# One tile's two store segments on two DMA queues, at the end of a fused attention and expert kernel

## The chip, the cores and the metric

The kernel runs on one core of a Trainium2 chip. Time is the device's time for one execution, in microseconds; the time before is the median of three runs.

## The reference

Sparse attention over 8 batches, 8 heads, 576 positions and 64 columns a head is followed by a two-layer network with an ELU between its layers:

```
scores = scale * q @ k.T                       # per batch and head
mask   = local (0 <= i-j < 32) for heads 0..3, strided ((i-j) % 32 == 0, i >= j) for heads 4..7
attn   = softmax(where(mask, scores, -1e9))
x      = (attn @ v) as [4608 tokens, 512]      # 8 batches of 576 tokens, heads side by side
h      = x @ w_in                              # [4608, 2048]
g      = where(h > 0, h, exp(min(h, 0)) - 1)
out    = g @ w_out                             # [4608, 512], float32
```

## The kernel before

Tokens are handled within a batch in an order of their own: token `p * 8 + s` of a batch stands at place `s * 72 + p`. There are 72 rows for each of the eight `s`, 576 for a batch. Chunks of 512 such places (9 of them) go through the two layers. Layer 1 (line 605) gives 16 blocks of 128 columns, which ScalarE and VectorE (DVE) turn into `g`. Layer 2 (line 639, token `Z`) multiplies `g` by `w_out` for one tile of 128 places at a time: four tiles a chunk, named `chunk.tile`, so 8.3 is the last tile of the last chunk. Its 128 x 512 result lies in a PSUM bank; a copy (line 645, by ScalarE with token `o`, by DVE with token `q`) brings it into an output tile `osb`, from a pool of four buffers, and `store` (token `t`) writes it to memory.

Since a tile of 128 places runs across the 72-row boundaries, `store` cuts it into two or three segments and issues one DMA for each (line 657). `engs` lists the queues, taken by turns; by default that is SyncE's (SP's) alone:

```
def store(ch, kk, engs=(nc.sync,), fs=slice(0, d_model)):
    ...
        n = min(RS - p, c0 + 128 - c)
        engs[i % len(engs)].dma_start(out=out_v[b, s, p:p + n, fs], in_=o_sb[c - c0:c - c0 + n, fs])
        c, i = c + n, i + 1
```

The last tile, 7.3, is computed and stored in three pieces: 256, 128 and 128 columns wide (`l2_piece`, token `Y`, line 669; `out_piece`, token `y`, lines 679 and 681). Piece 0 is copied by ScalarE and its two segments of 64 rows are stored from SP. Pieces 1 and 2 are copied by DVE, and of each the first segment is stored from SP, the second from ScalarE's queue.

The order of all this work is written out by hand in `ORDER`: a list of tokens that are run one after the other, each of which appends its instructions to its engines' programs. Every engine then runs its own instructions in that order and waits on semaphores where data, a buffer or a counter must be ready. SP's program holds nothing but DMA issues; ScalarE's holds its activations, its copies and the few DMAs issued from it. The stores of both queues count their landing on eight shared counters (named DMAHW0 to DMAHW7 in the built program), which the build gives out in turns. A store whose counter was used before waits until the earlier store on it has landed.

The last two lines of `ORDER` begin with the tiles of chunks 7 and 8 that are left; in them the copies `o.8.3`, `q.7.2`, `q.7.1`, `q.7.0`, `o.8.2` and then the three pieces of 7.3 follow each other.

Of the kernel before, what the change touches and what calls it, by code (L numbers as in the profile page):

```python
# [140 lines left out]
i.7.14 g.7.14 Z.7.2.0.6 h.7.4 i.8.8 j.7.8 Z.8.2.0.7 g.8.8 g.7.8 j.7.4 Z.8.0.0.4 g.8.10 L.8.15.1 g.7.4  # L141
Z.8.3.1.2 h.8.15 i.8.15 Z.8.0.1.4 g.8.15 Z.8.2.1.7 Z.8.1.0.5 Z.7.2.1.6 Z.8.1.1.5 Z.7.1.0.3 Z.8.1.2.5
Z.8.0.2.4 Z.7.2.2.6 Z.8.1.3.5 Z.8.0.3.4 o.8.1 Z.7.0.1.0 o.8.0 t.8.0 Z.8.3.2.2 Z.7.1.1.3 t.8.1 Z.7.1.2.3
Z.8.3.3.2 Z.7.2.3.6 o.8.3 t.8.3 Z.7.0.2.0 q.7.2 Z.7.1.3.3 t.7.2 Z.7.0.3.0 q.7.1 Z.8.2.2.7 t.7.1 q.7.0
Z.8.2.3.7 t.7.0 Y.7.3.0.6 o.8.2 t.8.2 y.7.3.0 Y.7.3.1.5 y.7.3.1 Y.7.3.2.4 y.7.3.2
"""

# [2 lines left out]
def kernel(  # L150
# [9 lines left out]
    nc = tc.nc  # L160
# [20 lines left out]
    g = [consts.tile([128, MC, CHUNK], BF16, tag=f"g{i}", name=f"g{i}") for i in range(2)]  # L181
# [433 lines left out]
    def clamp(eng, ch, m):  # L615
        i = int(ch), int(m)
        e = tiles.pop(("he", i))
        e1 = p_he1.tile([128, CHUNK], BF16, tag="he1", name="he1")
        if eng is nc.scalar:
            nc.scalar.activation(e1, e, ACT.Relu, bias=1.0, scale=-1.0)  # L620
        else:
            eng.tensor_scalar(e1, e, scalar1=1.0, scalar2=1.0, op0=ALU.min, op1=ALU.subtract)  # L622
        tiles["he1", i] = (e1, eng is nc.scalar)
# [19 lines left out]
    def copy_o(eng, ch, kk):  # L643
        o_sb = tiles["osb", ch, kk] = p_osb.tile([128, d_model], F32, tag="osb", name="osb")
        eng(o_sb, tiles.pop(("o", int(ch), int(kk))))  # L645
# [3 lines left out]
    def store(ch, kk, engs=(nc.sync,), fs=slice(0, d_model)):  # L649
        o_sb = tiles["osb", ch, kk]  # L650
        c0 = int(ch) * CHUNK + int(kk) * 128
        c, i = c0, 0
        while c < c0 + 128:
            b, r = divmod(c, S)
            s, p = divmod(r, RS)
# [3 lines that stand above are left out]
# [15 lines left out]
    def out_piece(ch, kk, i):  # L674
# [15 lines left out]
        "a": lambda ch, m, bk: l1(ch, m, (2, 3), bk), "b": lambda ch, m: l1(ch, m, (0, 1)),  # L690
        "L": lambda ch, m, bk: l1(ch, m, (2, 3, 0, 1), bk), "h": exp_h,
        "i": lambda *a: clamp(nc.vector, *a), "j": lambda *a: clamp(nc.scalar, *a),
        "g": elu, "Z": l2, "t": store, "Y": l2_piece, "y": out_piece,
        "o": lambda *a: copy_o(nc.scalar.copy, *a),
        "q": lambda *a: copy_o(nc.vector.tensor_copy, *a),
    }
# [33 lines left out]
```

## Time and profile before

| | us |
|---|---|
| median of 3 runs | 307.64 (307.57 to 308.14) |
| the profiled execution | 308.06 |
| its span, first to last instruction | 306.3 |
| TensorE busy | 294.3 (96%) |
| ScalarE busy | 228.6 (75%) |
| DVE busy | 227.3 (74%) |
| stores issued from SP after 289 us | 24, first at 289.1, last at 303.57 |
| stores issued from ScalarE | 2, at 300.94 and 301.84 |

The profile is of one execution; its span lies 1.7 us below that execution's own time. Durations in the text are from it. In a timeline a row has the start, the duration, the engine, the line and the operation, and in brackets the engine's idle time before it with what ended it. SPq and ACTq are DMA issues by SyncE and ScalarE; the transfer itself happens later on the 16 DMA engines, so an issue's row says nothing of when the data has landed.

### The profile page before, as it was taken

The page shows a single profiled execution, that of the slowest core. Times are in us where ns is not written, and L with a number is a line of the kernel's source. Part 1 is how long each engine was busy: PE and PEld are TensorE (multiplying, and loading weights), DVE is VectorE, ACT ScalarE, POOL GpSimd, SP SyncE. Part 2 cuts the span into 40 slices and gives each one's busy share as a digit, 9 for nine tenths or more (in the row PEclk, how much of TensorE's full clock was granted, in tenths as well). Part 3 has the DMA queues.
Part 4 walks back from the last instruction along what each step waited for, and adds up shares of the span by engine and source line. Part 5 has one row for each costly group of instructions (what it writes and reads, how often), then busy time and mean ns, then how long its engine had stood idle before and what let it go on. Part 6 is the DMA issues. An engine that isn't in the chain of part 4 may idle for free.

```text
span 306.3 us, 6219 instructions
## 1 busy us (share of the span) xinstructions
PE 294.3 (96%) x2299; PEld 146.8 (48%) x2339; DVE 227.3 (74%) x435; ACT 228.6 (75%) x412; POOL 81.7 (27%) x110
## 2 busy tenths in 40 slices
PE   6999999999999999999999999999999999999993
PEld 2654455445544454545544554454444544444453
DVE  6877959798779978896788878976788468894020
ACT  4778678588879888997989889978786659881110
POOL 8943336630472008530178240000000000000000
PEclk9999999999999999999999999999999999999999
DMA  8999999999999859999899599601120022000143
GB/s 164 184 206 206 207 193 166 153 196 207 169 153 168 127 118 134 162 193 159 203 149 155 65 138 167 166 26 46 37 68 0 2 68 68 2 1 0 28 150 98
DMA packets 107278, 37.59 MB, mean 123 GB/s; under 512 B 89104, under 2 KB 102768, under 8 KB 107248
## 3 DMA queue, kind: packets, MB, share of 16 engines
q0 software_dynamic: 69648, 19.43, 62.9%
q1 hardware_dynamic: 37088, 17.38, 27.8%
q10 hardware_dynamic: 512, 0.39, 0.5%
q8 instruction: 18, 0.29, 0.4%
q14 instruction: 12, 0.10, 0.1%
HBM read 39.47 MB, written 9.44 MB: 160 GB/s over the span
## 4 chain that ended last, share of the span: by engine, by line
PE 86%; DVE 6%; ACT 2%; issue 2%; DMA 2%; ACTq 0%; DVEq 0%
PE ps L639 39%; PE ps L605 36%; PE ps L450 3%; DVE g L633 2%; PE ps L520 2%; PE ps L513 2%; DVE he L622 2%; DMA g<-in_k_dram 2%; PE ps L669 1%; ACT he L613 1%; DVE mask_l L349 1%; DVE xT L578 1%; PE ps L493 0%; ACT e L457 0%; PE ps L408 0%
## 5 line engine op out<-in xcount | busy, mean ns | idle before, releaser
L639 PE MATMUL ps<-w_out_sb,g 128*128 128x512 bf16 x538 | 129.6, 379 | 2.0 <-issue 0.6
L605 PE MATMUL ps<-xT,w_in_sb 128*128 128x512 bf16 x559 | 129.4, 379 | 1.6 <-issue 0.3
L613 ACT ACTIVATE he<-ps 128x512 f32<-128x512 f32 x144 | 81.0, 597 | 22.2 <-PE ps L605 19.9
L605 PEld LDWEIGHTS <-w_in_sb 128*128 128x128 bf16 x576 | 55.0, 98 | 64.9 <-issue 1.7
L639 PEld LDWEIGHTS <-g 128*128 128x128 bf16 x560 | 51.1, 98 | 55.6 <-issue 0.6
L633 DVE TENSOR_TENSOR g<-he,ps 128x512 bf16<-128x512 bf16 x92 | 62.0, 684 | 1.9
L578 DVE TENSOR_TENSOR xT<-ps,ln 64x576 bf16<-64x576 f32 (+1 forms) x64 | 42.5, 677 | 19.7 <-ACT ln L553 18.9
L457 ACT ACTIVATE e<-ps 72x576 bf16<-72x576 f32 (+1 forms) x64 | 39.1, 647 | 13.4 <-PE ps L450 11.7
L622 DVE TENSOR_SCALAR he<-he 128x512 bf16<-128x512 f32 x92 | 40.1, 445 | 7.7 <-ACT he L613 7.0
L548 ACT ACTIVATE ln<-ps 64x576 f32<-64x576 f32 (+1 forms) x64 | 36.3, 583 | 9.8 <-PE ps L520 4.9
L631 DVE SCALAR_TENSOR_TENSOR g<-he,ps 128x512 bf16<-128x512 bf16 x52 | 34.8, 682 | 7.2 <-ACT he L620 6.9
L553 ACT ACTIVATE ln<-ln 64x576 f32<-64x576 f32 (+1 forms) x64 | 38.5, 619 | 1.2
L620 ACT ACTIVATE he<-he 128x512 bf16<-128x512 f32 x52 | 32.5, 630 | 1.6 <-DVE g L633 1.1
L645 DVE COPY osb<-ps 128x512 f32<-128x512 f32 x22 | 15.1, 685 | 16.3 <-PE ps L639 16.0
L239 POOL DMA_DIRECT2D ql<-in_q_dram x24 | 19.9, 833 | 6.8 <-DMA vl<-in_v_dram 3.1
L645 ACT COPY osb<-ps 128x512 f32<-128x512 f32 x13 | 7.6, 586 | 18.0 <-PE ps L639 14.1
L246 POOL DMA_DIRECT2D kl<-in_k_dram x24 | 17.8, 745 | 11.9 <-DMA w_out_sb<-in_moe_w_out_dram 4.0
L470 DVE TENSOR_TENSOR pm<-e,mask_l 128x576 bf16<-128x576 bf16 x32 | 14.1, 454 | 7.0 <-ACT e L457 5.4
L464 DVE TENSOR_TENSOR pm<-e,mask_s 72x576 bf16<-72x576 bf16 x32 | 14.2, 450 | 4.3 <-ACT e L457 4.1
L233 POOL DMA_DIRECT2D vs<-in_v_dram x8 | 5.2, 653 | 26.4 <-DVE vsp L585 25.2
L256 POOL DMA_DIRECT2D vl<-in_v_dram x8 | 9.6, 1195 | 8.7 <-PE ps L520 6.4
L513 PEld LDWEIGHTS <-vsp 72*128 72x128 bf16 x192 | 9.1, 98 | 5.4 <-DVE pm L464 0.3
(93 smaller groups left out, 156.1 us busy)
## 6 DMA issues: line engine op xcount, KB each, us to landing
out_dram<-osb SPq DMA_DIRECT2D x32, 144.0 KB
vl<-in_v_dram POOLq DMA_DIRECT2D x8, 288.0 KB, 8.8
w_in_sb<-in_moe_w_in_dram POOLq DMA_DIRECT2D x4, 512.0 KB, 13.0
w_out_sb<-in_moe_w_out_dram POOLq DMA_DIRECT2D x4, 512.0 KB, 16.3
kl<-in_k_dram POOLq DMA_DIRECT2D x24, 72.0 KB, 7.7
ql<-in_q_dram POOLq DMA_DIRECT2D x24, 72.0 KB, 8.8
ks<-in_k_dram POOLq DMA_DIRECT2D x5, 320.0 KB, 8.4
vs<-in_v_dram POOLq DMA_DIRECT2D x5, 320.0 KB, 8.6
```

What stands on the lines that cost most here:

```text
L457: nc.scalar.activation(e[0:R], tiles.pop(("S", key, u))[0:R], ACT.Exp, scale=scale)
L548: nc.scalar.activation(t, s_ps, ACT.Ln)
L553: nc.scalar.activation(t, t, ACT.Exp, scale=-1.0)
L578: nc.vector.tensor_mul(dst, o_ps, rc)
L605: nc.tensor.matmul(tiles["h", ch, m], lhsT=w_in_sb[:, c, m * 128:(m + 1) * 128], rhs=xT[:, c, ch * CHUNK:(ch + 1) * CHUNK], start=(c == 2) ...
L613: nc.scalar.activation(e, tiles["h", i[0], i[1]], ACT.Exp)
L620: nc.scalar.activation(e1, e, ACT.Relu, bias=1.0, scale=-1.0)
L622: eng.tensor_scalar(e1, e, scalar1=1.0, scalar2=1.0, op0=ALU.min, op1=ALU.subtract)
L631: nc.vector.scalar_tensor_tensor(dst, e1, -1.0, h, op0=ALU.mult, op1=ALU.max)
L633: nc.vector.tensor_tensor(dst, e1, h, op=ALU.max)
L639: nc.tensor.matmul(ops, lhsT=g[ch % 2][:, m, kk * 128:(kk + 1) * 128], rhs=w_out_sb[:, m, :], start=(m == 0), stop=(m == MC - 1), skip_gro ...
L645: eng(o_sb, tiles.pop(("o", int(ch), int(kk))))
```

## The change

The tile 8.3 (places 4480 to 4607: the last 56 rows of `s` = 6 and the 72 rows of `s` = 7 of the last batch) is stored by a new token `u`, which calls `store` with the queues of SP and ScalarE by turns. Its first segment, 56 rows, goes on SP's queue as before; its second, 72 rows, goes on ScalarE's. Nothing else in the text of the kernel differs.

```
-Z.8.3.3.2 Z.7.2.3.6 o.8.3 t.8.3 Z.7.0.2.0 q.7.2 Z.7.1.3.3 t.7.2 Z.7.0.3.0 q.7.1 Z.8.2.2.7 t.7.1 q.7.0
+Z.8.3.3.2 Z.7.2.3.6 o.8.3 u.8.3 Z.7.0.2.0 q.7.2 Z.7.1.3.3 t.7.2 Z.7.0.3.0 q.7.1 Z.8.2.2.7 t.7.1 q.7.0
...
-        "g": elu, "Z": l2, "t": store, "Y": l2_piece, "y": out_piece,
+        "g": elu, "Z": l2, "t": store,
+        "u": lambda ch, kk: store(ch, kk, (nc.sync, nc.scalar)), "Y": l2_piece, "y": out_piece,
```

## The prediction

> **What bounds the kernel now.** I read the page first, for where the change lies in the span.
>
> ```profile
> span 306.3 us, 6219 instructions
> ...
> PE 294.3 (96%) x2299; PEld 146.8 (48%) x2339; DVE 227.3 (74%) x435; ACT 228.6 (75%) x412; POOL 81.7 (27%) x110
> ...
> PE   6999999999999999999999999999999999999993
> ...
> DMA  8999999999999859999899599601120022000143
> ```
>
> TensorE is busy for 96% of the span, and for nearly all of it nothing but TensorE counts. The last slice (7.7 us wide) is different: TensorE falls to 3 tenths and the DMA engines to 3. The edited tile is stored just ahead of it, so the next views are of that end. The chain of waits, last rows:
>
> ```profile
> 297.94 3.55 PE ps L669 x48
> 301.49 0.02 issue
> 301.51 0.29 DVE osb L679
> ```
>
> The last computation ends at 301.51 + 0.29 = 301.80; the span ends at 306.3. These 4.5 us hold only stores and the closing barrier. Here the bound is the last store's issue and landing. The timeline, from the first store of the last tile, by engine (start, duration, engine; SPq and ACTq are the DMA issues of SyncE and ScalarE):
>
> ```profile
> 300.12 0.47 SPq L657 DMA_DIRECT2D out_dram<-osb  x1
> 300.64 0.59 SPq L657 DMA_DIRECT2D out_dram<-osb  x1
> 303.00 0.47 SPq L657 DMA_DIRECT2D out_dram<-osb  x1
> 303.57 0.54 SPq L657 DMA_DIRECT2D out_dram<-osb  x1
> ...
> 300.94 0.54 ACTq L657 DMA_DIRECT2D out_dram<-osb  x1
> 301.84 0.47 ACTq L657 DMA_DIRECT2D out_dram<-osb  x1
> ...
> 300.62 0.29 DVE L679 COPY osb<-ps 128x128 f32<-128x128 f32 x1 [3.67 <-PE ps L669]
> 301.51 0.29 DVE L679 COPY osb<-ps 128x128 f32<-128x128 f32 x1 [0.60 <-PE ps L669]
> ```
>
> The last tile (7.3) leaves in three pieces: piece 0 by two stores from SP (300.12, 300.64), pieces 1 and 2 each by one store from SP and one from ScalarE. Piece 1 is copied by 300.62 + 0.29 = 300.91. ScalarE stores its half at once (300.94). SP is free at 300.64 + 0.59 = 301.23, yet stores its half only at 303.00, and piece 2's half behind it at 303.57, although that was ready at 301.80. SP's own list of waits between 301 and 304 us says why:
>
> ```profile
> SPq L657 <- DMA out_dram<-osb: 1.7, 1, 1.7
> ```
>
> SP waits 1.7 us for another store to land. Which one, the order of the two built programs tells, with what each instruction waits for. Each store counts up one of eight counters DMAHW0 to 7, given out in turns over both queues, in the order in which the build expects the stores to be issued; before a counter is used again, the store that had it must have landed. First before, then after (rows left out at "..."):
>
> ```
> ## SP: 125 rows
> ...
> 106 L657 DMACopy out_0_dram<-osb_3948 56x512 [waits DMAHW4_49,Activation_49]
> 107 L657 DMACopy out_0_dram<-osb_3948 72x512 [waits DMAHW5_49]
> ...
> 115 L657 DMACopy out_0_dram<-osb_3978 72x512 [waits DMAHW5_49]
> 116 L657 DMACopy out_0_dram<-osb_3978 40x512 [waits DMAHW7_49]
> 117 L657 DMACopy out_0_dram<-osb_4003 40x512 [waits DMAHW0_49,Activation_49]
> 118 L657 DMACopy out_0_dram<-osb_4003 72x512 [waits DMAHW2_49]
> ...
> 122 L657 DMACopy out_0_dram<-osb_4008 64x128 [waits DMAHW6_49,DVE_49]
> 123 L657 DMACopy out_0_dram<-osb_4008 64x128 [waits DMAHW7_49,DVE_49]
> ```
> ```
> ## SP: 124 rows
> ...
> 106 L657 DMACopy out_0_dram<-osb_3948 56x512 [waits DMAHW5_49,Activation_49]
> ...
> 115 L657 DMACopy out_0_dram<-osb_3978 40x512 [waits DMAHW6_49]
> 116 L657 DMACopy out_0_dram<-osb_4003 40x512 [waits DMAHW0_49,Activation_49]
> 117 L657 DMACopy out_0_dram<-osb_4003 72x512 [waits DMAHW1_49]
> 118 L657 DMACopy out_0_dram<-osb_4003 16x512 [waits DMAHW3_49]
> ...
> 121 L657 DMACopy out_0_dram<-osb_4008 64x128 [waits DMAHW6_49,DVE_49]
> 122 L657 DMACopy out_0_dram<-osb_4008 64x128 [waits DMAHW7_49,DVE_49]
> ```
>
> Before, SP's turns go 5, 7, 0, 2: counters 6 and 1 went to ScalarE's two stores. So counter 6, for which SP's piece 1 store (row 122) waits, is that of ScalarE's piece 1 store, issued at 300.94; the wait ends as that one lands, just ahead of 303.00. Two engines store halves of one piece, and by the round of eight one must wait for the other.
>
> **The change part by part.** The 128 rows of tile 8.3 fall into two segments (56 and 72 rows). The first stays on SP, the second goes to ScalarE's queue. The rows around it:
>
> ```profile
> 292.80 0.59 ACT L645 COPY osb<-ps 128x512 f32<-128x512 f32 x1 [3.73 <-DMA out_dram<-osb]
> 298.02 0.59 ACT L645 COPY osb<-ps 128x512 f32<-128x512 f32 x1 [4.64 <-PE ps L639]
> ...
> 293.41 0.32 SPq L657 DMA_DIRECT2D out_dram<-osb  x1
> 293.77 0.37 SPq L657 DMA_DIRECT2D out_dram<-osb  x1
> 294.38 0.32 SPq L657 DMA_DIRECT2D out_dram<-osb  x1
> ...
> 293.66 0.69 DVE L645 COPY osb<-ps 128x512 f32<-128x512 f32 x1 [13.76 <-PE ps L639]
> ```
>
> 1. Removed from SP: one issue of 0.37 us at 293.77. SP's next store (294.38) starts only when DVE's copy ends, at 293.66 + 0.69 = 294.35; SP was free at 294.14. So SP gets 0.37 us of idle time and no later store moves: worth 0.
>
> 2. Added to ScalarE: one issue right behind its copy, from 293.39. Its price lies between 0.37 (the same store on SP) and 0.54 (ScalarE's dearer issue); I take 0.5, done by 293.9. Behind it on ScalarE stand the copy at 298.02, which waits for TensorE, piece 0's copy and the two stores of 7.3. The cover is 298.02 − 293.9 = 4.1 us of idle ScalarE; without it the 0.5 would go into the end. The copy at 298.02 also needs the four-deep output buffer that this tile gives back, so its landing matters: ScalarE's store of 300.94 had landed by 303.00, 2.06 us; from 293.4 that gives 295.5, 2.5 us early. Worth 0.
>
> 3. The counters. One store that the build expects earlier, on an idle queue, turns the round by a place. After, SP's turns go 6, 0, 1, 3: ScalarE's last stores have counters 7 and 2. SP's piece 1 store now waits for counter 6, that of tile 7.0's last segment, long landed; its piece 2 store, the very last, waits for counter 7, ScalarE's piece 1 store. So the wait doesn't go, it moves back by one store:
> - SP's piece 1 store is issued when SP is free, 301.23 + 0.05 (the gap between 300.12 + 0.47 and 300.64) = 301.28, no longer at 303.00.
> - SP's piece 2 store is ready at 301.80, and waits for the same landing as before: issued at 303.00 instead of 303.57. That is 0.57 us.
> - It no longer stands right behind another issue: 0.47 instead of 0.54, 0.07 more.
>
> Sum: 0.57 + 0.07 = 0.64 us. The packets confirm the distance of the last two stores. The DMA view in the windows 304.0 to 304.7 (slices of 0.0175 us) and 304.7 to 306.3 (0.04 us):
>
> ```profile
> DMA  0000000224547667664121100000000000000000
> ...
> DMA  0144664200000000000000000004000000000000
> ...
> q1 hardware_dynamic: 80, 0.03, 7.8%
> q14 instruction: 1, 0.01, 1.2%
> ```
>
> The first store moves its data from 304.12 to about 304.40, the second from 304.74 to 305.02: 0.62 apart. The lone packet later is of another queue. From the last data packet to the span's end are 1.3 us, of landing and barrier, and they follow the last store whenever it comes.
>
> 4. What may eat it: SP's piece 1 issue (301.28 to about 301.85) now overlaps ScalarE's piece 1 issue (300.94 to 301.48) by 0.2 us, and the last store hangs on that one's landing. Before, ScalarE's issue overlapped SP's of 300.64 by 0.29 us; the two took 0.59 and 0.54 where a lone one takes 0.47 (303.00, 301.84). So 0.3 us of overlap cost at most 0.12; 0.2 us cost up to 0.08, and nothing if ScalarE's descriptors are by then all made. The bounds are 0 and, if the landing is pushed by a whole issue, 0.47. I take 0.02, since the overlap falls in the last third of that issue. The other rows of this end, ScalarE's 301.84 among them, keep their times: DVE and TensorE aren't touched.
> The Trainium skill's page "Perfetto Trace Analysis", section "DMA Instruction — HWDGE (DVE, Sync)", says that the sequencers which issue such DMAs share one descriptor generator. The stretched 0.59 and 0.54 agree; taken as strict turns, it would eat the bound of 0.47 and leave 0.17 us of gain.
>
> Net: 0.64 − 0.02 = 0.62 us. The profiled execution took 308.06 us by the device (span 306.3 and 1.7 around it); it would take 307.44. The median of the runs is 307.64, 0.42 lower, and no step above depends on that distance: 307.64 − 0.62 = 307.02.
>
> **The rivals.**
> Hidden anyway, 307.64: reading SP alone, the removed 0.37 us lies in front of a wait for DVE (step 1), 12 us ahead of the end. If the order of landing made counters meaningless for the end (the 303.00 wait being on something else that stays), nothing moves. For it speaks that no view names the store waited for; against it, that the only long wait of SP coincides with a counter owned by ScalarE in the build, and that this owner changes.
> The Trainium skill's page "DMA: Bandwidth & Descriptors", section "Issuing engines are not separate DMA queues", says that issuing from several engines saves only the sequencer's issue time. By that rule alone the change saves 0.37 us on SP in front of an idle stretch, that is this rival; the 1.7 us row shows a second coupling, through the counters, that the rule doesn't treat.
>
> A slower end: the last store now depends on ScalarE's piece 1 store, whose issue lies between two of SP's. If descriptors are made one store at a time with SP's first, it comes out behind both, each 0.59 at most: 1.18 later than alone. It had at most 0.12 of that before; so the last store would go out 1.06 later than my 303.00, and 1.06 − 0.64 = 0.42 us are lost: 308.06. It decides from a landing 0.64 us later than before. Against it: ScalarE's 0.54 beside SP's 0.59 shows two issues side by side, not in turns.
>
> A partial gain, inside the forecast's case: 0.17 to 0.5 us, where step 4 costs more than I take.
>
> **How the numbers follow.** A difference of 0.2% (0.62 us) is about what a measurement of this kernel can tell from no change, and my gain stands on that line. Forecast case 0.80, hidden 0.12, slower 0.08. Of the forecast case I put 0.52 above the line, since the sum of 0.64 comes from rows and only step 4 takes from it, and 0.28 below, with the partial gains. That gives faster 0.52, same 0.28 + 0.12 = 0.40, slower 0.08. The likeliest case's own range is 306.85 to 307.47: the sum by step 4's bound above, and 0.17 under the forecast for the scatter of a median (the three runs span 307.57 to 308.14). The range reaches on to the hidden case, to 307.66, and to 306.80 for that scatter.
>
> **What would show it.** In the profile after: SP's piece 1 store at about 301.3 instead of 303.00; a wait of about 1.2 us (from 301.85) on a store's landing in front of SP's last issue, now at 303.0 to 303.1; its packets alone from about 304.1; the last data packet, and the span, some 0.6 us earlier; a 72-row issue on ScalarE at 293.4, and SP's 294.38 unmoved. I am wrong if SP's last issue is still near 303.57, if ScalarE's store of 300.94 lands after 303.6, or if a row before 300 us moves.

## The result and the profile after

The changed kernel takes 306.82 us (median, 306.24 to 307.82) against 307.57 (306.93 to 308.28) for the kernel before: ratio 0.9977, 95% interval 0.9968 to 0.9987, that is 0.71 us less (0.40 to 0.98). The forecast was 0.62 us less.

The profiled execution took 306.47 us, 1.59 less than the one of before. Most of that isn't the change's, as the span's two parts show. The page, and the timeline of the end (start, duration, engine; the ACT row is the copy of tile 8.3, just ahead of the edited store):

```profile
span 304.8 us, 6219 instructions
```
```profile
292.45 0.32 SPq L657 DMA_DIRECT2D out_dram<-osb  x1
293.43 0.32 SPq L657 DMA_DIRECT2D out_dram<-osb  x1
...
299.17 0.47 SPq L657 DMA_DIRECT2D out_dram<-osb  x1
299.68 0.59 SPq L657 DMA_DIRECT2D out_dram<-osb  x1
300.38 0.54 SPq L657 DMA_DIRECT2D out_dram<-osb  x1
302.04 0.47 SPq L657 DMA_DIRECT2D out_dram<-osb  x1
...
292.46 0.65 ACTq L657 DMA_DIRECT2D out_dram<-osb  x1
299.99 0.55 ACTq L657 DMA_DIRECT2D out_dram<-osb  x1
300.88 0.47 ACTq L657 DMA_DIRECT2D out_dram<-osb  x1
...
291.84 0.59 ACT L645 COPY osb<-ps 128x512 f32<-128x512 f32 x1 [3.73 <-DMA out_dram<-osb]
...
300.56 0.29 DVE L679 COPY osb<-ps 128x128 f32<-128x128 f32 x1 [0.60 <-PE ps L669]
```

The last DVE copy ends at 300.85, against 301.80 before: 0.95 us earlier. That much lies ahead of the edit: the copy of tile 8.3, which the edited store follows, already begins at 291.84 instead of 292.80. It is scatter between executions: another kernel below, whose program differs from this one only in which of two tiles in the last 17 us goes by two queues, has the last copy at 302.03 instead of 300.56. What the change can reach is read from the end of the last copy. To the span's end (304.76, and 306.34 before, to two places) it takes 304.76 − 300.85 = 3.91 us, against 306.34 − 301.80 = 4.54 before. That is 0.63 us less; the medians differ by 0.75, with the interval above.

Within these 3.91 us the wait has moved by one store. SP's piece 1 store goes at 300.38, 0.47 us ahead of the copy's end (before: 1.20 behind it); piece 2's waits, and goes 1.19 us behind it (before: 1.76). SP's list of waits at the end:

```profile
SPq L657 <- DMA out_dram<-osb: 1.1, 1, 1.1
SPq L726 <- DMA out_dram<-osb: 0.7, 1, 0.7
```

The 1.7 us for a landing are now 1.1, and they stand in front of the last issue alone. The second row is the wait for the last store itself, at the close of the program.

The views don't name the store waited for, but the trace also keeps the time at which each counter is counted up. In the kernel before, SP's wait ahead of 303.00 is on the counter that ScalarE's piece 1 store has; the last count of that store falls at 302.94, and SP's wait ends 0.02 us later. In the change the wait ahead of 302.04 is again on the counter of ScalarE's piece 1 store, whose last count falls at 301.98.

### The profile page after: what moved, and what is told of

Its sections match the earlier page's. It is cut to its first block, busy times and chain, and to the rows that moved or that the text cites. A ratio compares the mean times of both kernels' runs of the same rounds, so it can differ in the third digit from the quotient of the medians.

```text
span 304.8 us, 6219 instructions
## 1 busy us (share of the span) xinstructions
PE 293.6 (96%) x2299; PEld 146.6 (48%) x2339; DVE 226.4 (74%) x435; ACT 228.5 (75%) x412; POOL 81.6 (27%) x110
## 4 chain that ended last, share of the span: by engine, by line
PE 71%; DMA 21%; POOL 3%; issue 2%; DVE 2%; POOLq 0%; SPq 0%
PE ps L639 34%; PE ps L605 30%; DMA xT<-in_k_dram 6%; DMA qs<-in_q_dram 5%; DMA qTl<-ql 3%; DMA ql<-in_q_dram 3%; DMA w_in_sb<-in_moe_w_in_dram 3%; PE ps L450 3%; PE ps L520 2%; PE ps L513 2%; PE ps L669 1%; DVE g L633 1%; POOL ql L239 1%; POOL vs L233 0%; POOL ql L233 0%
## 5 line engine op out<-in xcount | busy, mean ns | idle before, releaser
L622 DVE TENSOR_SCALAR he<-he 128x512 bf16<-128x512 f32 x92 | 39.0, 432 | 7.7 <-ACT he L613 7.1
```

## The experiments

Theory: the counters. SP waits where a counter comes round that ScalarE's piece 1 store still holds; which store of SP that is follows from the order in which the build expects the stores of both queues, so that one store fewer or more on SP's queue ahead of it turns the round. Rivals: taking 8.3's segment off SP is itself what gains (issue time, or room ahead of 7.2), or the difference isn't the change's.

All figures in the table count from the end of the last DVE copy, in the profiled execution; "to the end" is up to the span's end. The ratio is to the kernel before, run beside each.

| kernel | SP's piece 1 store | SP's last store | to the end | median, ratio (95%) |
|---|---|---|---|---|
| before | 1.20 | 1.76 | 4.5 | 307.57 |
| the change | −0.47 | 1.19 | 3.9 | 306.82, 0.9977 (0.9968 to 0.9987) |
| 8.0 instead of 8.3 | −0.47 | 1.21 | 3.9 | 306.92, 0.9988 (0.9975 to 1.0) |
| 8.3 and 7.2 | −0.47 | 0.17 | 3.5 | 306.43, 0.997 (0.9958 to 0.9982) |
| one store more | 1.58 | 2.22 | 5.9 | 308.73, 1.0048 (1.0036 to 1.0061) |
| 8.3, and one more | 1.20 | 1.77 | 5.4 | 308.34, 1.0032 (1.002 to 1.0044) |
| seven tiles | −0.47 | 0.17 | 3.0 | 305.86, 0.9953 (0.9939 to 0.9966) |
| seven, and piece 0 | −0.87 | 0.03 | 3.1 | 306.17, 0.9957 (0.9944 to 0.9969) |
| seven, and one more | −0.48 | 0.17 | 3.4 | 306.3, 0.9967 (0.9955 to 0.998) |

**Another tile.** `u` stores by turns, as in the change.

```
-... o.8.0 t.8.0 ...
+... o.8.0 u.8.0 ...        # 8.3 keeps t
```

> Tile 8.0 (4.5 us earlier) is stored by turns from SP and ScalarE, 8.3 again from SP alone. Counter theory: one store fewer in SP's list turns the round of counters by the same place, SP's piece 1 store waits for tile 7.0's last segment and piece 2's for ScalarE's piece 1 store; SP's last issue comes 0.57 us earlier against the last DVE copy, time as for the change, about 0.6 us under before (ratio 0.998). Rival, that it matters that 8.3 itself leaves SP's queue just ahead of 7.2: no gain, ratio 1.000.

SP's last two issues stand as in the change within 0.02 us, though 8.3 is stored from SP alone:

```profile
301.85 0.54 SPq L657 DMA_DIRECT2D out_dram<-osb  x1
303.53 0.47 SPq L657 DMA_DIRECT2D out_dram<-osb  x1
...
302.03 0.29 DVE L679 COPY osb<-ps 128x128 f32<-128x128 f32 x1 [0.60 <-PE ps L669]
```

The gain isn't bound to tile 8.3. The median is 0.51 us under before (0.4 by the ratio); the interval just reaches 1.0, so the trace carries this verdict rather than the time.

**Two tiles.**

```
-... o.8.3 t.8.3 ... q.7.2 ... t.7.2 ...
+... o.8.3 u.8.3 ... q.7.2 ... u.7.2 ...
```

> Tiles 8.3 and 7.2 are both stored by turns: two stores fewer on SP. Counter theory: the round turns by one more place, no store of tile 7.3 waits for one of ScalarE's any more; SP's piece 2 issue comes when SP is free behind piece 1's, about 0.1 us after the end of the last DVE copy instead of 1.2 us, and the time falls by 0.6 + 1.1 = 1.7 us against before (ratio 0.9945). Rival, that each issue taken off SP is worth some 0.4 to 0.6 us by itself: 0.8 to 1.2 us (ratio 0.996 to 0.9975). Rival hidden anyway: nothing beyond the change.

SP's last store goes at 0.17 (0.1 was expected): no store of 7.3 waits for ScalarE's. Its row, and its last copy's:

```profile
301.08 0.55 SPq L657 DMA_DIRECT2D out_dram<-osb  x1
...
300.62 0.29 DVE L679 COPY osb<-ps 128x128 f32<-128x128 f32 x1 [0.60 <-PE ps L669]
```

But of the 1.0 us by which it moved against the change, only 0.4 reached the end, and the time fell by 1.0 us instead of 1.7. Of the 0.65 us lost, 0.15 are a longer landing (1.92 us from the start of the issue to the last count, 1.77 in the change), and 0.5 lie behind the landing. The theory of the counters holds for the issue; what follows the last store is not the fixed 1.3 us that the prediction assumed. By the time alone the first rival (0.8 to 1.2 us) would fit as well; against it stand the issue at 0.17 and, below, a kernel with 8.3 moved that gains nothing.

**One store more.** The middle segment of 8.0 is cut, all stores stay on SP.

```
-            n = min(RS - p, c0 + 128 - c)
+            n = min(RS - p, c0 + 128 - c, most)      # most=48 for tile 8.0, else 128
```

> All stores from SP as before, but the middle segment of tile 8.0 is cut into 48 and 24 rows, one more issue of 0.3 us on SP at about 290 us, where SP idles for 2 us right behind. Counter theory: the round turns the other way, piece 0's second store on SP now waits for ScalarE's piece 1 store, and three stores stand behind that wait instead of two: SP's last issue comes 0.55 to 0.6 us later, time 0.6 us over before (ratio 1.002). Rival, SP's issue time alone: hidden in the idle stretch, ratio 1.000.

The wait goes the other way, to piece 0's second store, with three stores behind it:

```profile
302.27 0.47 SPq L657 DMA_DIRECT2D out_dram<-osb  x1
302.84 0.54 SPq L657 DMA_DIRECT2D out_dram<-osb  x1
303.48 0.54 SPq L657 DMA_DIRECT2D out_dram<-osb  x1
...
300.97 0.29 DVE L679 COPY osb<-ps 128x128 f32<-128x128 f32 x1 [0.60 <-PE ps L669]
```
```profile
SPq L657 <- DMA out_dram<-osb: 2.2, 1, 2.2
```

A cut that costs SP some 0.3 us where it idles for 2 makes the kernel 1.3 us slower, where the theory expected 0.6. 0.46 us of that is the last store (2.22 instead of 1.76); the other 0.9 us come behind it.

**8.3 by turns, and one more.** Both edits; SP has as many stores as before.

> The change (8.3 by turns) and the cut of tile 8.0's middle segment together: SP has as many stores as before. Counter theory: the counters of tile 7.3 stand as before, SP's piece 1 store waits for ScalarE's again, time as before (ratio 1.000) though 8.3 has its two queues. Rival, that moving 8.3's segment is itself what gains: 0.6 us under before (ratio 0.998).

```profile
302.77 0.47 SPq L657 DMA_DIRECT2D out_dram<-osb  x1
303.33 0.54 SPq L657 DMA_DIRECT2D out_dram<-osb  x1
...
300.71 0.55 ACTq L657 DMA_DIRECT2D out_dram<-osb  x1
...
301.27 0.29 DVE L679 COPY osb<-ps 128x128 f32<-128x128 f32 x1 [0.60 <-PE ps L669]
```

SP's issues stand where they stood before, to 0.01 us, with 8.3 moved: the move itself gains nothing. Yet the kernel is 0.9 us slower than before, where the theory expected no difference, and 0.8 us of it again lie behind the last store. The closing waits of SP (the rows of the program's end, by line; count, durations in ns, first to last start) show them. This kernel, from the last landing on:

```profile
L727 SPq EVENT_SEMAPHORE  x6: 27/28/28, 305.2 to 305.6; - x6
...
L727 SPq EVENT_SEMAPHORE  x2: 28/28/28, 306.0 to 306.0; - x2
```

The kernel before, its only closing wait from the last landing on, and the change's:

```profile
L725 SPq EVENT_SEMAPHORE  x1: 28/28/28, 305.4 to 305.4; - x1
```
```profile
L726 SPq EVENT_SEMAPHORE  x1: 28/28/28, 303.8 to 303.8; - x1
```

SP closes by waiting for one counter after the other, 0 to 7, some 0.06 us each. With one store more the round ends one place further: the last store has counter 0, and eight waits are still to come when it lands (305.2 to 306.0); before and after the change it has counter 7, the last in the list, and one is left. In the eight stands a gap, from 305.6 to 306.0. Counted in SP's rows of the trace it comes ahead of row 207 (the first is 0) here, with two tiles and with one more, 0.37 to 0.38 us each, whatever stands there. In the kernel before it stands there too (0.37 us), and the wait for the last landing right behind covers it; in the change row 207 is that wait itself. With two tiles moved it falls behind the last landing, between the last closing wait and the drain:

```profile
L727 SPq EVENT_SEMAPHORE  x2: 28/28/28, 303.0 to 303.1; - x2
L727 SPq DRAIN  x1: 130/130/130, 303.5 to 303.5; - x1
```

So there are two theories for what follows the last store: the order of the closing waits, and a pause at a place in SP's program. Two of the next three kernels tell them apart.

**Seven tiles.** All of `t.8.1 t.8.0 t.8.3 t.7.2 t.7.1 t.7.0 t.8.2` become `u`.

> All seven tiles 8.1 to 8.2 ahead of 7.3 are stored by turns: seven issues fewer on SP than before, five fewer than with two tiles moved. The stores of 7.3 have the same counters free as with two moved, so SP's last issue stays about 0.1 to 0.2 us behind the last DVE copy. Theory of a pause at a place in SP's program: in six traces a gap of 0.36 to 0.38 us (or more, where a landing ends later) stands ahead of SP's row 207 of the trace, whatever that is; here SP has only 207 rows (0 to 206), so the pause is gone from the end, and from the last copy to the span's end it takes 3.1 us instead of 3.53 with two moved (3.91 for the change, 4.54 before). Rival, that the gap belongs to the drain that follows the last landing: 3.5 us again. Time: 1.3 us under before (ratio 0.9957) by the first, 1.0 by the second.

```profile
301.03 0.55 SPq L657 DMA_DIRECT2D out_dram<-osb  x1
...
300.57 0.29 DVE L679 COPY osb<-ps 128x128 f32<-128x128 f32 x1 [0.60 <-PE ps L669]
```

The last store stands as with two tiles (0.17); to the end it takes 3.0 us instead of 3.5, and no gap of 0.36 us stands among the last rows but those of landings and the barrier. The closing order is the same as with two tiles, so the pause went with the number of SP's rows (207 here, 212 there). This kernel has the lowest median of all: 305.86 us, ratio 0.9953, 1.6 us under the kernel before beside it (307.44).

**Seven, and piece 0 by turns.**

```
-        store(ch, kk, (nc.sync,) if i == "0" else (nc.sync, nc.scalar), slice(f0, f1))
+        store(ch, kk, (nc.sync, nc.scalar), slice(f0, f1))
```

> As with seven moved, and piece 0 of tile 7.3 by turns too: SP has one issue for each piece of 7.3 and is free when piece 2 is copied. Its last issue comes 0.03 us behind the last DVE copy instead of 0.15, alone on SP at 0.47 to 0.55; last landing 0.1 to 0.25 us earlier, so 2.85 to 3.0 us from the last copy to the end, time 1.5 us under before (ratio 0.995). Rival, that two issues at once cost as much as the two in a row: the same as with seven moved.

```profile
300.73 0.47 SPq L657 DMA_DIRECT2D out_dram<-osb  x1
...
300.73 0.51 ACTq L657 DMA_DIRECT2D out_dram<-osb  x1
...
300.41 0.29 DVE L679 COPY osb<-ps 128x128 f32<-128x128 f32 x1 [0.60 <-PE ps L669]
```

SP's last store goes 0.14 us earlier and the end doesn't (3.1 us; the two times' intervals overlap). The rival holds: SP and ScalarE issue piece 2 at the same moment, and their stores land one behind the other. By the counters, SP's lands 1.82 us behind the last copy's end and ScalarE's 2.09; with seven tiles, where ScalarE issues first, it was ScalarE's at 1.83 and SP's at 2.08.

**Seven, and one more.** Seven tiles by turns, 8.0's middle segment cut as above, its third and fourth part on SP.

> As with seven moved, but tile 8.0's middle segment is cut in two (48 and 24 rows), one store more: the round of counters ends one place further, the very last store has counter 0 instead of 7. Closing-wait theory: SP's closing waits go through the counters in the order 0 to 7, with 0.06 us each; where the last store has counter 0, seven of them are still to come when it lands, 0.45 us more than with seven moved (3.6 instead of 3.1 us from the last copy to the end), and the pause ahead of SP's row 207 falls into the last barrier row or is gone. Rival, that the closing waits cost nothing since they run while others land: no difference from seven moved.

The issues stand as with seven tiles; to the end it takes 0.4 us more (3.4 us, 3.6 were expected):

```profile
L728 SPq EVENT_SEMAPHORE  x8: 28/28/28, 303.1 to 303.5; - x8
```

Eight closing waits after the landing, without a gap among them, 0.4 us from first to last. The closing order alone is worth this; in the kernel with 8.3 and one more, pause and order together were worth 0.8.

## Why the prediction was right

Step 1 (SP's freed 0.37 us are worth nothing): 7.2's first store still waits for DVE's copy; 293.43 is 7.42 us ahead of the last copy's end, as 294.38 was before.

Step 2 (ScalarE's issue is covered): it took 0.65 us at 292.46, over the bound of 0.54 (it starts 0.01 us behind SP's), and nothing behind it moved. The price, taken at 0.5, was wrong by 0.15 and hidden by 4 us of idle ScalarE. The landing was taken at 2.06 us and took 2.77 (from 292.46 to the last count at 295.23), so the output buffer was free 1.8 us ahead of the copy that needs it (297.02), not 2.5.

Step 3 (the counters): the terms came out as summed. The last issue moved by 1.76 − 1.19 = 0.57 us and took 0.47 instead of 0.54. That the counters cause it, and not the move, is shown by the counts above, which name the store waited for, and from four sides by the kernels: the same gain by another tile, no gain in the issues with 8.3 moved and a store added, a later wait with a store added, and no wait with two moved.

Step 4 (overlap): taken at 0.02, bounded by 0.47. ScalarE's piece 1 issue took 0.55 instead of 0.54, it landed 1.99 us after its start instead of 2.00, and the wait for its landing ended 0.01 us earlier against the last copy; the overlap cost nothing that the trace shows, and the slower end, which needed a landing 0.64 us later, is out. The bound of 0.47 supposed that SP's piece 1 issue could push ScalarE's. SP's starts 0.39 us behind ScalarE's here, so the run shows only that a later issue didn't push an earlier one. Where both start together ("seven, and piece 0"), ScalarE's store took 2.06 us to land instead of 1.80. Issues that overlap are longer here (0.59 and 0.55 beside 0.47; 0.65 beside 0.37 for the same 72 rows on SP), but so is one right behind another of its own queue (0.54 at 303.57, before), so the stretch isn't the overlap's alone. The Trainium skill's page "Perfetto Trace Analysis" (section "DMA Instruction — HWDGE (DVE, Sync)") has one generator shared by the issuing sequencers. The landings one behind the other agree with it; turns in order of arrival are not excluded by any run here, and in the change they would cost the last store nothing.

The hidden-anyway rival, which is what the page "DMA: Bandwidth & Descriptors" of the Trainium skill gives (section "Issuing engines are not separate DMA queues"), is right for the issue on SP and misses the time, since it doesn't treat the counters.

One assumption held by luck. "1.3 us, of landing and barrier" were said to follow the last store whenever it comes. In the change they do, because the number of stores and so the last counter is unchanged and the pause is still covered by the last landing. With two tiles moved the assumption failed by 0.5 us, with a store added by 0.8 to 0.9.

## What to carry to other kernels

Where stores of several queues share a few completion counters, a store can wait for one it has nothing to do with: list, from the built program, which earlier store holds the counter of each of the last issues, and look whether that one is still in flight. Any edit that adds, splits or moves a store can turn the round, so its effect on the end may have either sign whatever the edit costs where it stands. At the very end also ask what the closing waits still have to go through when the last store lands.

## What was not expected of the hardware

A pause of 0.37 us stands ahead of SP's row 207 in the trace of each kernel that has that row outside a longer wait, and isn't seen in the kernels with 206 or 207 rows, which end ahead of it; with 208 rows it would fall on the last barrier row, whose gap is the usual 0.46 us. Its cause isn't settled; that it comes and goes with the number of SP's rows is what the runs show. A fetch of instructions is an obvious candidate, but in the gaps with two tiles, with one store more, and with 8.3 and one more, the trace has no packet of any DMA queue, the instruction queues among them. Two small stores issued at the same moment from SP and ScalarE end no sooner than two of which one follows the other by 0.14 us: in both cases the later one lands 2.1 us behind the last copy's end, some 0.26 us behind the other.
